# Another placing of the recurrence blocks and of ScalarE's and VectorE's work around them, in an mLSTM and MLP kernel

## The chip, the cores and the metric

One core of one Trainium2 chip runs the program. The metric is the device time of one execution in microseconds; the median of the runs counts. The profile is that of one execution, and its times are those of that execution.

## What is computed

A recurrence over 768 time steps for 4 batches and 8 heads (an mLSTM with exponential gates, a matrix memory C of 40 by 40 and a normalizer n for each head), and behind it an MLP with a SiLU gate on the 3072 tokens of 320 features, with 2048 hidden units:

```python
for t in range(S):                     # q, k, v: (4, 8, 768, 40)
    m_new = np.maximum(f_gate[:, :, t] + m, i_gate[:, :, t])
    f_stab = np.exp(f_gate[:, :, t] + m - m_new)
    i_stab = np.exp(i_gate[:, :, t] - m_new)
    C = f_stab * C + i_stab * einsum('bhd,bhe->bhde', v_t, k_t)
    n = f_stab * n + i_stab * k_t
    y[:, :, t] = sigmoid(o_gate_t) * (C @ q_t) / np.maximum(np.abs(n . q_t), 1.0)
x = y.transpose(0, 2, 1, 3).reshape(3072, 320)
h = x @ w_in                            # 320 x 2048
out = (h * sigmoid(h)) @ w_out          # 2048 x 320
```

## The kernel before

The recurrence is cut into 12 chunks of 64 time steps and 2 pairs of batches: 24 units of 128 tokens, in order. Unit n needs the state `Cm` of unit n-2. Three units make a step of 384 tokens, and there are eight steps. The MLP of a step goes through 16 groups of 128 hidden units. The main loop (line 1298) counts groups of all steps through, k = 18 to 128, with k // 16 the step and k % 16 the group.

In a turn k of that loop TensorE gets, in this order: the first product of group k (`first_product`: w_in by x, split into a high and a low part, so that a product is three products); a second product (`second_product`: the activations by w_out, in the same three parts) for groups four or more back; in an even turn the first product is cut in two and a second product lies between. All these matmuls use 64 rows of the array, and two of them on different row halves run beside each other: the first half of group k beside the second half of group k-1. Where two halves add to the same PSUM tile, one must have ended before the other starts. `relay` and `follow` see to that by a wait that passes through ScalarE's list: `relay` puts an empty instruction on ScalarE behind a matmul, `follow` makes a later matmul wait for it. `first_product` of turn k waits in that way for `rises[k - 2]`, the tanh of group k-2.

ScalarE and VectorE make the activations of group k-1 in turn k: `rise` (tanh `th` from the PSUM tile `spot`, line 916, on ScalarE; (th + 1) times `spot`, line 919, on VectorE, which frees that PSUM tile) and `part` (the high part `gh`, line 928, ScalarE; the low part `gl`, line 932, VectorE). `gh` and `gl` have four buffers each. There are three PSUM tiles called `spot`.

While a step's groups run, the three units of the next step are worked into it, each by a block at a given group (`PLACES`, line 41): in step 1 and later at groups 3, 7 and 11. `at[a]` in the loop is the unit whose block was `a` turns ago. In the block's own turn TensorE does, between the first and the second product, the scores of unit n+1 (line 570), the values of unit n (641, 658) and the state product of unit n (732), which takes the two free `spot` tiles. Then `close` (VectorE: `weigh` multiplies the scores of n+1, `norm` makes the denominators), `part`, `hold` (ScalarE copies the state product out as `pk`, line 761, and gives the two `spot` tiles back), `level` and `scale` (VectorE, which make x), `carry` step 0 (GpSimd), `turn_out` (VectorE transposes 32 by 32 blocks, line 798) and `turn_away` (SyncE starts four stores of x to DRAM, line 804). One turn later: `carry` step 1 (VectorE, four additions to `Cm`, line 792), and `turn`, in which SyncE starts the loads of unit n+3 (lines 476, 485, 505, 496) and of `lq` of unit n+2 (line 517) and GpSimd makes `am`. Two turns later: `add` (GpSimd), `misc` of unit n+1 (`gate` and `look` on ScalarE, lines 543 and 550, and `near` on GpSimd, line 554, which makes `qt`), and `turn_in` (SyncE loads x back transposed as `px`, line 812). Three turns later the exponential of unit n+2 (540) and `keys`. Six turns later, and for the third unit of a step four turns later, `xput`: ScalarE casts `px` to `xh` (841) and VectorE makes `xl` (842), which the first products of the next step read.

Each engine has its own list of instructions and they are in the order in which the code issues them (the order is written out by hand, there is no scheduler). The same holds for SyncE's DMA starts. The output of a step, three tiles of 128 tokens, is finished in groups 2 and 3 of the next step (`store`: ScalarE copies it out of PSUM, line 988, and SyncE starts two stores of it, line 993).

## Time and profile before

| | |
|---|---|
| time, median of 3 runs | 486.35 us (486.13 to 487.97) |
| the profiled execution | 488.12 us, of which the span (first to last instruction) is 486.3 us |
| TensorE, matmuls | 443.9 us busy (91% of the span) |
| VectorE | 292.6 us (60%) |
| ScalarE | 220.5 us (45%) |
| GpSimd | 124.0 us (26%) |

PE is TensorE's matmul row, ACT is ScalarE, DVE VectorE, POOL GpSimd, SP SyncE, and a q behind a name is the engine's queue of DMA starts. Up to about 84 us the kernel is in its first loop (step 0); then the main loop runs, with the starts of steps 2 to 7 at about 134, 195, 254, 314, 376 and 431 us. Step 7 holds no blocks. A line such as `[1.46 <-ACT pk L761]` says that the engine had been idle for 1.46 us and that the instruction of ScalarE on line 761 that writes `pk` ended the wait.

### The profile page before, as it was taken

To read this page: it belongs to the slowest core of one execution; us is meant where nothing else is said; L and a number is where in the kernel's file an instruction comes from. 1 tells how busy PE (TensorE), PEld (TensorE's weight loads), DVE (VectorE), ACT (ScalarE), POOL (GpSimd) and SP (SyncE) were. 2 spreads that over 40 slices of the span, in tenths; PEclk is the share of its full clock that TensorE was granted. 3 is DMA by queue.
4 is the path that set the end of the run, shared out by engine and by line. 5 is a ranking of instruction groups with operands and counts; after the bars stand their busy time and mean duration, and the time that the engine had idled before them with its cause. 6 is when DMAs were issued, how large, how long until landed. Compare 5 with 4: busy or idle time off the path is not lost.

```text
span 486.3 us, 16335 instructions
## 1 busy us (share of the span) xinstructions
PE 443.9 (91%) x6814; PEld 398.3 (82%) x6814; DVE 292.6 (60%) x647; ACT 220.5 (45%) x487; POOL 124.0 (26%) x136
## 2 busy tenths in 40 slices
PE   8999999999798996989969899798988989989996
PEld 5767777888698986989859888698977989989996
DVE  5798986678826675366652666536655355644342
ACT  7776677455623444233443334434424324434332
POOL 6733441343103441034410344104341031100000
PEclk9999999999979999899998999999979889999999
DMA  8999892255602646035650356604555031101001
GB/s 264 388 332 265 254 278 84 69 148 150 161 1 67 156 146 161 1 86 136 151 155 4 86 135 154 155 14 118 130 122 144 8 84 25 35 18 42 1 1 42
DMA packets 65402, 58.01 MB, mean 119 GB/s; under 512 B 33424, under 2 KB 51936, under 8 KB 65328
## 3 DMA queue, kind: packets, MB, share of 16 engines
q1 hardware_dynamic: 65056, 56.60, 42.5%
q8 instruction: 54, 0.88, 0.8%
q10 hardware_dynamic: 208, 0.26, 0.2%
q14 instruction: 20, 0.16, 0.1%
q0 software_dynamic: 64, 0.10, 0.1%
HBM read 49.28 MB, written 7.55 MB: 117 GB/s over the span
## 4 chain that ended last, share of the span: by engine, by line
PE 59%; issue 17%; ACT 8%; DVE 7%; DMA 7%; SPq 1%; POOL 0%; POOLq 0%; ACTq 0%; DVEq 0%
PE spot L1263 20%; PE pout L1285 17%; PE ph L885 6%; PE pout L967 5%; DMA px<-xd 4%; PE p L570 2%; DVE th L919 2%; ACT gh L928 2%; PE p L658 2%; DMA vb<-in_vp_dram 2%; PE spot L732 1%; PE p L641 1%; DVE Cm L792 1%; ACT th L916 1%; DMA D<-LFl 1%
## 5 line engine op out<-in xcount | busy, mean ns | idle before, releaser
L1263 PE MATMUL spot<-xh,wh 64*128 64x384 f32 x660 | 122.9, 363 | 28.8 <-ACT xh L841 17.6
L919 DVE SCALAR_TENSOR_TENSOR th<-th,spot 128x384 f32<-128x384 f32 x110 | 60.7, 552 | 80.7 <-ACT th L916 80.2
L916 ACT ACTIVATE th<-spot 128x384 f32<-128x384 f32 x110 | 53.7, 488 | 119.0 <-PE spot L1263 119.0
L1285 PE MATMUL pout<-woh,gh 64*128 64x320 f32 x648 | 106.7, 321 | 0.0
L1285 PE MATMUL pout<-wol,gh 64*128 64x320 f32 x648 | 104.6, 315 | 2.2 <-issue 1.3
L1285 PE MATMUL pout<-woh,gl 64*128 64x320 f32 x648 | 104.5, 314 | 0.0
L932 DVE TENSOR_TENSOR gl<-th,gh 128x384 fp32r<-128x384 f32 x112 | 66.0, 589 | 57.3 <-ACT gh L928 56.8
L928 ACT CAST gh<-th 128x384 fp32r<-128x384 f32 x112 | 57.4, 513 | 93.9 <-DVE th L919 66.5
L1263 PE MATMUL spot<-xl,wh 64*128 64x384 f32 x550 | 98.8, 348 | 0.9 <-issue 0.4
L1263 PEld LDWEIGHTS spot<-xh,wh 64*128 64x128 f32 x660 | 65.2, 191 | 40.1 <-ACT xh L841 19.2
L1263 PE MATMUL spot<-xh,wl 64*128 64x384 f32 x440 | 77.7, 344 | 0.0
L782 POOL TENSOR_TENSOR Cm<-Cm,lq 40x328 f32<-40x328 f32 x40 | 30.0, 751 | 149.6 <-PE p L658 148.0
L1285 PEld LDWEIGHTS pout<-wol,gh 64*128 64x128 f32 x648 | 65.2, 193 | 2.8 <-issue 1.6
L1285 PEld LDWEIGHTS pout<-woh,gh 64*128 64x128 f32 x648 | 64.9, 193 | 1.6 <-issue 0.7
L1285 PEld LDWEIGHTS pout<-woh,gl 64*128 64x128 f32 x648 | 65.1, 193 | 0.0
L554 POOL TENSOR_TENSOR qt<-qk,lq 104x512 f32<-104x512 f32 x22 | 29.1, 1323 | 124.5 <-ACT lq L550 112.8
L1263 PEld LDWEIGHTS spot<-xl,wh 64*128 64x128 f32 x550 | 55.5, 193 | 2.5 <-DVE xl L842 2.3
L1263 PEld LDWEIGHTS spot<-xh,wl 64*128 64x128 f32 x440 | 44.1, 193 | 0.0
L967 PE MATMUL pout<-wo,g 128*128 128x320 f32 x96 | 29.0, 436 | 0.0
L537 POOL TENSOR_TENSOR D<-D,am 128x512 f32<-128x512 f32 x20 | 26.8, 1339 | 6.5 <-DMA D<-LFd 4.5
L842 DVE TENSOR_TENSOR xl<-px,xh 128x384 fp32r<-128x384 f32 x18 | 18.8, 1043 | 13.6 <-ACT xh L841 13.6
L597 DVE TENSOR_TENSOR D<-p,D 128x512 f32<-128x512 f32 x24 | 16.5, 689 | 16.3 <-PE p L658 14.8
(160 smaller groups left out, 556.5 us busy)
## 6 DMA issues: line engine op xcount, KB each, us to landing
qk<-in_qk_dram SPq DMA_DIRECT2D x24, 512.0 KB, 5.3
ko<-in_ko_dram SPq DMA_DIRECT2D x24, 320.0 KB, 5.6
wro<-in_w_out_dram SPq DMA_DIRECT2D x8, 640.0 KB, 5.5
wri<-in_w_in_dram SPq DMA_DIRECT2D x8, 512.0 KB, 6.2
D<-LFl SPq DMA_DIRECT2D x32, 128.0 KB, 3.0
lq<-LFl SPq DMA_DIRECT2D x32, 128.0 KB, 5.0
vb<-in_vp_dram SPq DMA_DIRECT2D x48, 82.0 KB, 4.9
out_dram<-ob SPq DMA_DIRECT2D x45, 80.0 KB, 2.1
```

The costliest lines, as they stand in the source:

```text
L537: nc.gpsimd.tensor_tensor(out=self.Dm, in0=self.Dm, in1=self.am, op=ALU.add)
L554: nc.gpsimd.tensor_tensor(out=self.qt, in0=self.q[:KS], in1=self.lq[:KS], op=ALU.mult)
L782: nc.gpsimd.tensor_tensor(out=v, in0=v, in1=self.lq[r, :, L - 1].unsqueeze(2).broadcast_to([D, H, D1]), op=ALU.mult,)
L842: nc.vector.tensor_tensor(out=lo, in0=px[:, a, :], in1=hi.bitcast(F32), op=ALU.subtract)
L885: nc.tensor.matmul(ph, w, x, start=(i == 0), stop=(i == len(ops) - 1))
L916: self.tanh = nc.scalar.activation(th, ph, AF.Tanh, scale=0.5)
L919: nc.vector.scalar_tensor_tensor(out=th, in0=th, scalar=1.0, in1=ph, op0=ALU.add, op1=ALU.mult)
L928: nc.scalar.copy(gh, th)
L932: nc.vector.tensor_tensor(out=gl, in0=th, in1=gh.bitcast(F32), op=ALU.subtract)
L967: nc.tensor.matmul(self.po[t], g[:, ts], w, start=(fc == 0 and i == 0), stop=(last and i == len(ops) - 1), skip_group_check=(j == NSTEP - 1),)
L1263: m = nc.tensor.matmul(spot[g][:, :NT], *ops[i], start=(h == 0 and i == 0), stop=(h == 1 and i == n - 1), skip_group_check=True,)
L1285: m = nc.tensor.matmul(st.po[t], g[half(h), t * UT : (t + 1) * UT], w[half(h)], start=(f == 0 and i == 0 and (p, h) in ((0, 0), (0, 1), (1 ...
```

## The change

Seven things are changed.

- `PLACES`: from step 2 on the blocks lie at groups 1, 5 and 9, in step 1 still at 3, 7 and 11.
- `gh` and `gl` get five buffers instead of four.
- In `part`, `gl` is made ahead of `close`, and no longer behind it.
- Unit 8, the third of step 2, no longer goes through DRAM: it is left out of `AROUND`, so TensorE transposes its x in the turn after its block (`xpose`, line 830, three transposes) and `xput` follows at once.
- Work moves between turns. `misc` of unit n+1 goes from two turns after the block to the end of the block's own turn. `turn` and `add` follow in the next turn, directly behind `carry`, of which the first half now stands ahead of `part`. Stores 1 and 0 go ahead of `relay`, store 2 goes behind `part`. `turn_in` is issued ahead of `xput`.
- `first_product`: the wait for the tanh of group k-2 hangs on the first matmul of the second half (h = 1), and not on the first matmul of all.
- In the first even turn of a step's second product, five pieces of the first product stand ahead of it instead of four.

```diff
@@ -38,7 +38,7 @@
 NWT = 3
 
 EARLY = 7
-PLACES = ((5, 9, 12), (3, 7, 11))
+PLACES = ((5, 9, 12), (3, 7, 11), (1, 5, 9))
 FIRST = NFC + LAG
 LAST = NSTEP * NFC - 1
 
@@ -62,7 +62,7 @@
     cp = pool("cp", 1)
     p2 = pool("p2", 2)
     p3 = pool("p3", 3)
-    p4 = pool("p4", 4)
+    p5 = pool("p5", 5)
     pb = pool("pb", NBIG)
     pw = pool("pw", NWT)
     psO = pool("psO", 3, space=PSUM)
@@ -767,12 +767,12 @@
                 nc.scalar.copy(t[r, 1], self.pu[1][r])
             self.pu[1] = t[:, 1]
 
-        def carry(self, copy=nc.scalar.copy, steps=(0, 1)):
+        def carry(self, copy=nc.scalar.copy, steps=(0, 1), parts=(0, 1)):
             n, c, p = self.n, self.c, self.p
             if c == NC - 1:
                 return
             pu = self.pu
-            for a in range(2):
+            for a in parts:
                 r = slice(a * 64, a * 64 + D)
                 v = Cm[p][r, a, :].rearrange("p (h e) -> p h e", e=D1)
                 if c == 0:
@@ -895,7 +895,7 @@
                 next(x)
             if j == 0:
 
-                g = p4.tile([128, NT], F32, tag="gh", name=f"g{j}_{fc}")
+                g = p5.tile([128, NT], F32, tag="gh", name=f"g{j}_{fc}")
                 nc.vector.scalar_tensor_tensor(
                     out=g, in0=th, scalar=1.0, in1=ph, op0=ALU.add, op1=ALU.mult
                 )
@@ -908,7 +908,7 @@
                 out=th, in0=th, scalar=1.0, in1=ph, op0=ALU.add, op1=ALU.mult
             )
             self.th = th
-            self.part(fc, splits, between)
+            self.part(fc, splits, lambda: None, between)
 
         def rise(self, fc, splits):
             j, ph = self.j, spot[self.j * NFC + fc][:, :NT]
@@ -921,18 +921,19 @@
             )
             free.append(spot.pop(j * NFC + fc))
 
-        def part(self, fc, splits, between):
+        def part(self, fc, splits, between, ahead=lambda: None):
             j, th = self.j, self.th
-            gh = p4.tile([128, NT], F32R, tag="gh", name=f"gh{j}_{fc}")
-            gl = p4.tile([128, NT], F32R, tag="gl", name=f"gl{j}_{fc}")
+            gh = p5.tile([128, NT], F32R, tag="gh", name=f"gh{j}_{fc}")
+            gl = p5.tile([128, NT], F32R, tag="gl", name=f"gl{j}_{fc}")
             nc.scalar.copy(gh, th)
             for x in splits:
                 next(x, None)
-            between()
+            ahead()
             nc.vector.tensor_tensor(
                 out=gl, in0=th, in1=gh.bitcast(F32), op=ALU.subtract
             )
             self.g[fc] = (gh, gl)
+            between()
 
         def rows(self, fc, half):
 
@@ -994,7 +995,7 @@
 
 
     units = [Unit(n) for n in range(NU)]
-    AROUND = set(range(2 * UPS, NU))
+    AROUND = set(range(2 * UPS, NU)) - {3 * UPS - 1}
     free, spot = [], {}
     steps = {}
 
@@ -1203,7 +1204,7 @@
         j, fc = divmod(k, NFC)
         if j >= NSTEP - 1:
             return {}
-        return {fc - a: units[(j + 1) * UPS + u] for u, a in enumerate(PLACES[min(j, 1)])}
+        return {fc - a: units[(j + 1) * UPS + u] for u, a in enumerate(PLACES[min(j, 2)])}
 
     def splits(k):
         return [SPLITS[x[0]](int(x[1])) for x in LOWS.get(divmod(k, NFC), ())]
@@ -1267,8 +1268,9 @@
                     stop=(h == 1 and i == n - 1),
                     skip_group_check=True,
                 )
-                follow(m, turn)
-                turn = None
+                if h == 1:
+                    follow(m, turn)
+                    turn = None
         return m
 
     def second_product(p, k, turn=None):
@@ -1306,9 +1308,10 @@
             first_product(k, 0, 8, last_turn)
             last_turn = None
         elif even and ready:
-            first_product(k, 0, 4, rises[k - 2])
+            cut = 4 + (old % NFC == 0)
+            first_product(k, 0, cut, rises[k - 2])
             last_turn = relay(second_product(0, old, last_turn))
-            first_product(k, 4, 8)
+            first_product(k, cut, 8)
         else:
             first_product(k, 0, 8, rises[k - 2])
         new = steps[(k - 1) // NFC]
@@ -1318,13 +1321,15 @@
             rises[k - 1] = new.tanh
         if 0 in at:
             block(at[0].n)
+        last = steps[old // NFC] if ready and old % NFC == NFC - 2 else None
         if ready:
             m = second_product(1 if even else 2, old, last_turn)
             if 0 not in at:
+                if last:
+                    last.store(1 if even else 0)
                 last_turn = relay(m)
-            if old % NFC == NFC - 2:
-                for t in (1,) if even else (0, 2):
-                    steps[old // NFC].store(t)
+        if 1 in at:
+            at[1].carry(steps=(1,), parts=(0,))
         if k > FIRST:
             new.part((k - 1) % NFC, parts, (lambda: close(at[0].n)) if 0 in at else (lambda: None))
         if 0 in at:
@@ -1334,24 +1339,26 @@
             at[0].level()
             at[0].scale()
             at[0].carry(steps=(0,))
-            at[0].turn_out()
-            at[0].turn_away()
+            if at[0].n in AROUND:
+                at[0].turn_out()
+                at[0].turn_away()
+            if at[0].n + 1 < NU:
+                units[at[0].n + 1].misc()
+        if last and not even:
+            last.store(2)
         if 1 in at:
-            at[1].carry(steps=(1,))
-        if 2 in at and at[2].n + 1 < NU:
-            if at[2].n + 2 < NU:
-                units[at[2].n + 2].add()
-            units[at[2].n + 1].misc()
+            at[1].carry(steps=(1,), parts=(1,))
+            turn(at[1].n)
+            if at[1].n + 2 < NU:
+                units[at[1].n + 2].add()
         if 3 in at and at[3].n + 2 < NU:
             units[at[3].n + 2].exp()
             units[at[3].n + 2].keys()
-        if 1 in at:
-            turn(at[1].n)
+        if 2 in at and at[2].n in AROUND:
+            at[2].turn_in()
         for back in (4, 6):
-            if back in at and (at[back].n % UPS == UPS - 1) == (back == 4):
+            if back in at and at[back].n in AROUND and (at[back].n % UPS == UPS - 1) == (back == 4):
                 at[back].xput(steps[k // NFC + 1])
-        if 2 in at:
-            at[2].turn_in()
 
     st = steps[NSTEP - 1]
     st.mm2(NFC - 4)
```

## Rows read from the trace of the kernel before

**Rows 1.** The page: TensorE's busy time, share of the span and instructions.

```profile
PE 443.9 (91%) x6814; PEld 398.3 (82%) x6814; DVE 292.6 (60%) x647; ACT 220.5 (45%) x487; POOL 124.0 (26%) x136
```

**Rows 2.** Table of waits: engine, line, releaser: us in total, times, longest.

```profile
ACT gh L928 <- PE pout L1285: 26.0, 15, 2.5
...
PE spot L1263 <- ACT xh L841: 17.6, 6, 4.0
...
PE spot L1263 <- ACT pk L761: 9.8, 15, 1.5
...
ACT xh L841 <- DMA px<-xd: 5.7, 4, 1.7
...
PE spot L732 <- DVE th L919: 4.1, 6, 0.8
```

**Rows 3.** Timeline, TensorE, starts of steps 2, 4, 6: start, us, instruction [idle before].

```profile
134.14 0.69 PE L1263 MATMUL spot<-xh,wh 64*128 64x384 f32 x2 [2.85 <-ACT xh L841]
...
254.05 0.69 PE L1263 MATMUL spot<-xh,wh 64*128 64x384 f32 x2 [3.99 <-ACT xh L841]
...
375.79 0.59 PE L1263 MATMUL spot<-xh,wh 64*128 64x384 f32 x2 [2.15 <-ACT xh L841]
```

**Rows 4.** Busy time by stretch: length, PE, PEld, DVE, ACT, POOL (instructions), granted clock.

```profile
133.90:140.30 6.40, 6.16 (x40) 5.85 (x42) 1.11 (x2) 0.68 (x2) 0.00 (x0) 0.50 0.00 0
...
211.00:215.00 4.00, 3.98 (x48) 3.94 (x50) 2.83 (x7) 0.84 (x3) 1.67 (x2) 1.00 0.46 104
...
359.00:365.50 6.50, 5.92 (x40) 5.92 (x42) 2.36 (x7) 0.49 (x1) 2.55 (x3) 0.50 0.30 58
...
393.00:396.40 3.40, 3.40 (x26) 3.40 (x26) 2.75 (x6) 0.00 (x0) 0.66 (x1) 0.50 0.38 94
...
sum 15.50, PE 14.84 PEld 13.77 DVE 1.47 ACT 0.55 POOL 0.00; mean PE 3.71 PEld 3.44 DVE 0.37 ACT 0.14 POOL 0.00
```

**Rows 5.** Timeline, behind the first block of step 3.

```profile
209.61 0.77 ACT L988 ACTIVATE ob<-pout 128x320 f32<-128x320 f32 x2 [2.50 <-PE pout L1285]
...
210.26 0.51 ACT L928 CAST gh<-th 128x384 fp32r<-128x384 f32 x1
...
211.02 0.44 PE L1263 MATMUL spot<-xh,wh 64*128 64x384 f32 x2 [1.46 <-ACT pk L761]
```

**Rows 6.** Timeline, third block of step 3.

```profile
234.68 0.69 PE L570 MATMUL p<-qk 40*64 40x64 f32 x32
...
236.79 0.47 PE L732 MATMUL spot<-vb,kw 64*40 64x41 f32 x26 [0.67 <-DVE th L919]
...
238.82 0.44 PE L1263 MATMUL spot<-xh,wh 64*128 64x384 f32 x2 [0.22 <-ACT pk L761]
```

**Rows 7.** Timeline behind that block; below, the starts and landings of `lq`.

```profile
241.29 2.81 SPq L804 DMA_DIRECT2D xd<-xt  x4
...
241.48 0.49 ACT L916 ACTIVATE th<-spot 128x384 f32<-128x384 f32 x1 [2.52 <-PE spot L1263]
...
244.22 0.38 PE L1263 MATMUL spot<-xh,wh 64*128 64x384 f32 x2
...
249.22 0.55 SPq L812 DMA_DIRECT2D px<-xd  x1
...
253.49 0.51 ACT L841 CAST xh<-px 128x384 fp32r<-128x384 f32 x1 [1.71 <-DMA px<-xd]
...
L517 SPq DMA_DIRECT2D lq<-LFl x2: 602/604/607, 247.9 to 248.5; - x2
...
DMA to landing us min/median/max: 4.5/4.8/5.0
```

**Rows 8.** GpSimd's `qt` there; the durations of `xl`, ns, least, median, most.

```profile
246.93 1.30 POOL L554 TENSOR_TENSOR qt<-qk,lq 104x512 f32<-104x512 f32 x1 [5.13 <-DMA D<-LFl]
...
L842 DVE TENSOR_TENSOR xl<-px,xh x18: 551/1348/1366, 113.3 to 431.6; 128x384 fp32r<-128x384 f32 x18
```

**Rows 9.** TensorE's transposes in step 0: busy us, mean ns.

```profile
L830 PE MATMUL p<-ident,x 128*128 128x128 f32 x9 | 1.5, 273 | 0.0
```

## Prediction

> **What bounds the kernel now.** I read the page's engine times first: TensorE is busy for 91% of the span [rows 1], so what can be won is its idle time and the time in which it runs at the lower clock. The table of waits names the idle time [rows 2]: TensorE stood 17.6 us at six places for `xh` (once per start of a step from 2 on), 9.8 us at fifteen places for `pk` (the group behind each block waits for `hold`'s copies, which give back two PSUM tiles), and 4.1 us at six places inside blocks for `th` (the state products want the PSUM tile that `rise` frees). The timeline shows single waits: 2.85 at the start of step 2, 3.99 at that of step 4, 2.15 at that of step 6 [rows 3]. The table by stretch then shows the second half of the price: behind such a wait the granted clock is 0.50 (1.2 of 2.4 GHz) for 3 to 6 us, against 1.00 elsewhere, and 40 matmuls take 6.16 us where 48 take 3.98 [rows 4]. A half-clock stretch costs half its length: 3.1 us behind the start of step 2, 7.4 us in the four stretches 195 to 198.4, 253.6 to 259.1, 314.5 to 317.7 and 376 to 379.4 us together (the sum row: half of 14.84), 1.7 us at 393 us, where a 1.45 us wait for `pk` came before.
>
> **The change, part by part.** The sum is against the profiled execution (488.12 us, span 486.3). It stands 1.8 us above the median of 486.35; one stretch at 359 us, half clock for 6.5 us [rows 4], may belong to that execution alone, so I count nothing for it and take the sum off the median.
>
> *Waits behind blocks.* ScalarE's `gh` waited 26.0 us at fifteen places for second products [rows 2]: with four buffers it needs the one whose last reader is the second product queued behind the block. The fifth buffer's last reader ran two groups earlier. In the first block of a step two stores stand ahead of `gh` too (209.61, then `gh` 210.26), and TensorE waits 1.46 [rows 5]; in a third block 0.22 [rows 6]. From step 2 on the change moves the blocks away from the groups that store, and stores 0 and 1 now stand ahead of the relay in groups without a block. `pk` can then end before the second product does: 9.0 of 9.8 us go. The wait for `th` comes from a backlog of exponentials and x casts two groups ahead; part of that (`misc`) moves to another group: 2.0 of 4.1 us go, bounds 0 and 4.1.
>
> *Start of step 2.* Unit 8 leaves the way through DRAM (one DVE transpose, four stores, one load) for three TensorE transposes of 273 ns [rows 9], 0.8 us, and a wait for x and the cast that I bound by 0 and 2.85 us (the present wait) and take at 0.6: VectorE has `x` ready about when TensorE gets there, one group after the block. Removed: 2.85 and 3.1 of clock. Net 4.5 us gained.
>
> *Starts of steps 3 to 7.* They cost 17.6 - 2.85 = 14.75 us. With blocks at 1, 5, 9 the third unit's x is cast in group 13, not 15, so the starts themselves no longer wait. But ScalarE works its list in order, and the cast keeps its distance of four groups to the block while the DMA chain is as long as before: SyncE issues the four stores (241.29), seven loads and then `px` (249.22), and the cast starts at 253.49, after 1.71 us of waiting, 18.8 us after the block's first score matmul at 234.68 [rows 6, 7]. TensorE reached the end of that fourth group at 254.05 - 3.99 = 250.06 [rows 3], or 15.4 us after; without the 0.67 and 0.22 of rows 6 that is 14.5. It needs the tanh queued behind the cast at the first second-half matmul of group 15. A pair of groups takes 244.22 - 238.82 = 5.4 us [rows 6, 7], of which the even one, with two second products, has some 3.3: TensorE asks at 17.8 and gets the tanh at 18.8 + 0.51 + 0.49 = 19.8. That is a new wait of 2.0 us in group 15. ScalarE's four waits for `px` had a sum of 5.7, mean 1.4 [rows 2], and in step 5 there was none, so I take 1.5 us for each of steps 2 to 5 (bounds 0 and 3.0), and 0 in step 6, where no loads stand ahead of `px`. Net 14.75 - 6.0 = 8.75 us gained. The clock fell behind the start wait of 2.15 us and behind the 1.45 us before 393 us, but not behind the 1.46 us before 211 [rows 3 to 5]; so 1.5 us may go either way, and I keep half of the 7.4 us: 3.7 gained, and the 1.7 at 393 us.
>
> *`misc` two groups earlier.* ScalarE now does `gate` and `look` of unit n+1 at the end of block n. `look` needs `lq`, which was requested one group after block n-1: the second of its DMAs starts at 248.5 and lands up to 5.0 us later [rows 7], 18.6 to 18.8 us after the scores. Two pairs of groups and a block (10.8 + 2.5) separate two blocks and `look` comes 3.8 us into its block, so 17.1 us after the previous scores: it waits 1.5 us and ends 5.9 us into its block. The tanh queued behind it was due at 241.48 - 234.68 - 0.89 = 5.9, after 2.52 us of idle time [rows 6, 7]. So at the third block the idle time pays for it. At the second block two output DMAs now stand ahead of the loads in SyncE's queue, 0.6 us each like the `lq` issues of rows 7; the tanh is 1.2 us late, of which TensorE has 0.3 or 0.4 to spare: 0.8 us lost in each of four steps, 3.2 in all (bounds 0 and 10). All six output DMAs stand ahead of the first unit's `px`, 3.6 us; its cast comes six groups after its block, so this loses 0 to 2.4 us over the run; I take 1.0.
>
> *GpSimd beside VectorE.* `xl` takes 1.348 us in the median and 0.551 at best; it is long where `qt` runs on GpSimd (246.93) [rows 8]. The move frees `xl`, but `qt`, `am` and the addition now run beside `carry` and `gl`. I take 2.0 us lost over the run (bounds 0 and 10). The Trainium skill, "GPSIMD Engine Reference", section "8. Key points", says that the two engines share SBUF interfaces and that contention arises with VectorE instructions that have two SBUF inputs. The trace agrees for `xl`; by that rule `carry` and `gl` have the same exposure behind a block, which is the third rival.
>
> Priced at nothing: the cut of 5 instead of 4 (no wait stands there now), the wait hung on the first second-half matmul (one matmul sooner), the two halves of `carry` (the first fills VectorE's wait for `gh`), `gl` ahead of `weigh` (both start when the scores and `gh` are there; what follows shifts by under 0.4 us). If VectorE were full behind a block these would cost their 0.3 to 0.6 us each; it is the contention case.
>
> **Sum.** -9.0 - 2.0 - 4.5 - 8.75 - 3.7 - 1.7 + 3.2 + 1.0 + 2.0 = -23.5 us: 486.35 - 23.5 = 463.
>
> **Rivals.** *Hidden:* the loads land sooner relative to the groups, ScalarE never makes TensorE wait, the clock holds. Then 6.0, 3.7, 3.2, 1.0 and 2.0 come off as well: 447, or about 451 with some left. For: the spare is missed by 2 us in only one chain. Against: SyncE's issues are back to back in rows 7. *ScalarE waits longer:* 3.0 us in group 15 and 2 us at two blocks in four steps, the clock falling behind each group 15: 463 + 6 + 3.7 + 4 = 477. For: rows 7 make the wait likely; against: every TensorE delay gives the loads more time. *Contention:* each VectorE operation with two SBUF inputs waits behind one of GpSimd after a block, `gh` and the next tanh come 0.6 us late at 15 blocks: 463 - 2 + 9 = 470. *The waits only move:* the `pk` wait stays because tanh and `gh` become later, and group 15 takes the whole start wait: 486. *Slower:* three waits in each of steps 2 to 5 (second block, third block, group 15), all long enough that the half clock follows each. Twelve stretches at the mean of rows 4, 14.84 / 4 / 2 = 1.9 us, cost 22.3 instead of the 3.7 counted, and waits of 2.2 us each instead of 9.2 us in all cost 17 more: 499; with half the blocks spared 491. It decides if `lq` lands 1.5 us later than rows 7 say.
>
> **Chances.** The forecast 0.46, hidden 0.16, longer waits 0.15, contention 0.09, waits only move 0.06, slower 0.08. The range of 449 to 479 takes in the forecast, the contention, the longer waits and most of the hidden case. What this kernel's measurement can tell from no change is about 0.5% (2.4 us): faster 0.86, same 0.06, slower 0.08.
>
> **What would show it.** In the table of waits after: `spot` for `pk` near 1 us; `xh` no longer at step starts; a new TensorE wait for ScalarE's `th` in group 15 (1 to 2 us, four times) and a smaller one two groups behind the second block; ScalarE waiting for DMA at `look` and at `xh`; `xl` near 0.56 us; at 132 us no half clock. Wrong would be: `pk` waits of 1.4 us left, half clock in new places, or no ScalarE wait at group 13 (then the hidden case).

## The result and the profile after

The changed kernel takes 454.4 us in the median (452.9 to 454.9), the kernel before 486.2 beside it: a ratio of 0.934, with a 95% interval of 0.930 to 0.938. The forecast was 463 with a range of 449 to 479. The chip has a slower state that some executions fall into; the medians here take in such executions, the ratios leave them out. The profiled execution took 454.91 us, its span is 453.1. Lines have moved by one or two: the first product is L1264 now, the second L1287, the copy of the output L989.

TensorE's row of the page, to be held against [rows 1]:

```profile
PE 430.0 (95%) x6817; PEld 390.1 (86%) x6817; DVE 299.7 (66%) x646; ACT 224.4 (50%) x487; POOL 131.1 (29%) x136
```

The span is 33.2 us shorter. TensorE's idle time fell from 486.3 - 443.9 = 42.4 us to 453.1 - 430.0 = 23.1, which is 19.3 of them. Its busy time fell by 13.9, though the same products are made, so the clock comes next. Busy time by stretch: the two stretches of the main loop at half clock that are left, and the start of step 2, which ran at half clock before [rows 4] (columns as in rows 4):

```profile
184.00:187.80 3.80, 3.80 (x28) 3.80 (x30) 1.58 (x3) 1.32 (x3) 0.00 (x0) 0.55 0.00 0
225.00:228.80 3.80, 3.74 (x29) 3.74 (x30) 1.56 (x5) 0.99 (x2) 1.28 (x2) 0.56 0.17 28
```

```profile
132.00:138.00 6.00, 6.00 (x132) 5.75 (x129) 3.70 (x8) 2.98 (x6) 0.00 (x0) 1.00 0.00 0
```

Seven stretches of before held 6.16 + 14.84 + 5.92 + 3.40 = 30.3 us of matmuls at half speed [rows 4]; half of that, 15.2 us, is lost. Two are left, with 7.54 us at 0.55 of the clock, a loss of 3.4. So the clock gave 11.8 us, and 2.1 us are neither idle time nor clock. That last part shows in an undisturbed pair of groups: 5.35 us before, 5.30 after.

The table of waits, after (those of before are rows 2):

```profile
ACT xh L841 <- DMA px<-xd: 9.6, 3, 3.7
...
PE pout L1287 <- ACTq L1244: 6.7, 5, 2.3
...
ACT gh L928 <- PE pout L1287: 5.6, 6, 1.3
...
ACT lq L550 <- DMA lq<-LFl: 5.3, 3, 2.6
...
PE pout L1287 <- issue: 3.5, 4, 1.4
...
PE spot L1264 <- ACT pk L761: 0.5, 1, 0.5
PE spot L732 <- DVE th L919: 0.5, 1, 0.5
```

TensorE's waits for `xh` (17.6 us) are gone, those for `pk` fell from 9.8 to 0.5, those for `th` inside blocks from 4.1 to 0.5, and `gh` waits 5.6 us for second products instead of 26.0. Two lines are new. One is 6.7 us in which a second product waits for ScalarE's queue. That is the relay, an empty instruction behind which the second half may start. The other is ScalarE's wait for `px`, which was 5.7 us and is 9.6. They belong together, as the timeline at the end of step 2 shows:

```profile
183.90 0.51 ACT L841 CAST xh<-px 128x384 fp32r<-128x384 f32 x1 [3.70 <-DMA px<-xd]
...
183.98 0.63 PE L1287 MATMUL pout<-woh,gh 64*128 64x320 f32 x2 [2.30 <-ACTq L1244]
```

ScalarE stood 3.70 us before the cast of `px`. The relay of the second product stands behind the cast in its list, and TensorE stood 2.30 us, to 0.08 us after the cast began. The clock fell to half right there. The same pair stands at 293.46 and 293.54 (3.04 and 1.64 us) and at 346.95 and 347.03 (2.89 and 1.49), with the clock at 1.00 behind them. In step 3 there is none.

The second block of step 5 shows the other new wait, and what follows it:

```profile
320.62 0.63 ACT L550 ACTIVATE lq<-lq 104x512 f32<-104x512 f32 x1 [2.60 <-DMA lq<-LFl]
...
320.70 0.42 PE L1287 MATMUL pout<-woh,gh 64*128 64x320 f32 x2 [0.96 <-ACTq L1244]
...
321.38 1.30 POOL L554 TENSOR_TENSOR qt<-qk,lq 104x512 f32<-104x512 f32 x1 [3.03 <-ACT lq L550]
...
322.14 1.82 DVE L792 TENSOR_TENSOR Cm<-Cm,pk 40x164 f32<-40x164 f32 x2
...
322.65 1.13 POOL L529 TENSOR_TENSOR am<-mask,aT 128x512 f32<-128x512 f32 x1
...
323.85 1.73 POOL L537 TENSOR_TENSOR D<-D,am 128x512 f32<-128x512 f32 x1
...
324.46 1.56 DVE L792 TENSOR_TENSOR Cm<-Cm,pk 40x164 f32<-40x164 f32 x2
...
326.05 0.56 DVE L919 SCALAR_TENSOR_TENSOR th<-th,spot 128x384 f32<-128x384 f32 x1
...
326.63 0.51 ACT L928 CAST gh<-th 128x384 fp32r<-128x384 f32 x1 [2.85 <-DVE th L919]
...
326.71 0.42 PE L1287 MATMUL pout<-woh,gh 64*128 64x320 f32 x2 [0.33 <-ACTq L1244]
```

ScalarE waited 2.60 us for `lq`, TensorE 0.96 behind it. Then GpSimd runs `qt`, `am` and the addition to `D` without a break, and beside them VectorE's four additions of `carry` take 1.82 + 1.56 us where four take 1.15 when nothing runs beside them (b1, at 286.46). `th` and `gh` come late (`gh` stood 2.85 us), and TensorE stands another 0.33.

### The profile page after: what moved, and what is told of

Its sections match the earlier page's. It is cut to its first block, busy times and chain, and to the rows that moved or that the text cites. A ratio compares the mean times of both kernels' runs of the same rounds, so it can differ in the third digit from the quotient of the medians.

```text
span 453.1 us, 16196 instructions
## 1 busy us (share of the span) xinstructions
PE 430.0 (95%) x6817; PEld 390.1 (86%) x6817; DVE 299.7 (66%) x646; ACT 224.4 (50%) x487; POOL 131.1 (29%) x136
## 4 chain that ended last, share of the span: by engine, by line
PE 58%; issue 20%; DVE 10%; DMA 7%; ACT 2%; SPq 1%; POOL 0%; POOLq 0%; ACTq 0%; DVEq 0%
PE pout L1287 19%; PE spot L1264 18%; PE ph L885 7%; PE pout L968 6%; DVE Cm L792 4%; DMA px<-xd 3%; PE p L570 3%; PE p L658 2%; DVE th L919 2%; PE p L641 2%; DMA qk<-in_qk_dram 2%; PE spot L732 1%; DVE gl L932 1%; DMA ko<-in_ko_dram 1%; DMA lq<-LFl 1%
## 5 line engine op out<-in xcount | busy, mean ns | idle before, releaser
L1264 PE MATMUL spot<-xh,wh 64*128 64x384 f32 x660 | 138.7, 343 | 0.5 <-ACT pk L761 0.5
L1287 PE MATMUL pout<-woh,gh 64*128 64x320 f32 x648 | 121.0, 318 | 7.1 <-ACTq L1244 6.7
L1287 PE MATMUL pout<-woh,gl 64*128 64x320 f32 x648 | 117.1, 308 | 3.5 <-issue 3.5
L1287 PE MATMUL pout<-wol,gh 64*128 64x320 f32 x648 | 116.5, 307 | 1.6 <-DVE wol L337 1.6
L1264 PE MATMUL spot<-xl,wh 64*128 64x384 f32 x550 | 114.2, 338 | 0.0
L1264 PEld LDWEIGHTS spot<-xh,wh 64*128 64x128 f32 x660 | 89.6, 186 | 3.4 <-ACT th L916 1.3
L1264 PE MATMUL spot<-xh,wl 64*128 64x384 f32 x440 | 90.7, 336 | 0.0
L1287 PEld LDWEIGHTS pout<-woh,gh 64*128 64x128 f32 x648 | 78.0, 186 | 13.5 <-ACTq L1244 9.2
L1287 PEld LDWEIGHTS pout<-woh,gl 64*128 64x128 f32 x648 | 78.2, 186 | 2.8 <-issue 2.8
L1287 PEld LDWEIGHTS pout<-wol,gh 64*128 64x128 f32 x648 | 78.0, 186 | 1.9 <-DVE wol L337 1.9
L1264 PEld LDWEIGHTS spot<-xl,wh 64*128 64x128 f32 x550 | 70.2, 186 | 0.0
L1264 PEld LDWEIGHTS spot<-xh,wl 64*128 64x128 f32 x440 | 58.1, 186 | 0.0
L792 DVE TENSOR_TENSOR Cm<-Cm,pk 40x164 f32<-40x164 f32 x70 | 42.0, 634 | 0.5
L885 PE MATMUL ph<-x,wi 128*128 128x384 f32 x64 | 23.7, 492 | 0.3 <-DVE wi L301 0.3
## 6 DMA issues: line engine op xcount, KB each, us to landing
D<-LFl SPq DMA_DIRECT2D x32, 128.0 KB, 3.1
lq<-LFl SPq DMA_DIRECT2D x32, 128.0 KB, 4.9
```

What stands on the lines that cost most here:

```text
L792: nc.vector.tensor_tensor(out=w, in0=w, in1=pu[d][r], op=ALU.add)
L885: nc.tensor.matmul(ph, w, x, start=(i == 0), stop=(i == len(ops) - 1))
L1264: m = nc.tensor.matmul(spot[g][:, :NT], *ops[i], start=(h == 0 and i == 0), stop=(h == 1 and i == n - 1), skip_group_check=True,)
L1287: m = nc.tensor.matmul(st.po[t], g[half(h), t * UT : (t + 1) * UT], w[half(h)], start=(f == 0 and i == 0 and (p, h) in ((0, 0), (0, 1), (1 ...
```

## The experiments

All times are medians; a ratio is to the kernel before on the same chip, whose median there was 485 to 487 us. 0.01 of ratio is 4.9 us. Where a kernel isn't set against the changed one on the same chip, the ratios are compared (0.934 for the changed kernel in both of its measurements).

The table below is worked out from the start times of TensorE's timeline. It gives the time from the first second-product matmul of one even turn to that of the next, in us, summed over steps 2 to 5, so four pairs of groups in each column; the column's number is the first group of the pair within its step. An undisturbed pair gives 4 x 5.30 = 21.2, or 21.4 at 5.35. With the new places the blocks lie in columns 0, 4 and 8 and the px cast in 12 and 14; with the old ones the blocks lie in 2, 6 and 10 and the start of the next step in 14.

```
kernel              0     2     4     6     8    10    12    14    sum
before           27.0  36.8  21.4  32.1  22.2  38.4  23.2  40.5  241.7
b1_places_alone  32.6  21.4  33.0  21.6  38.0  22.2  25.8  22.2  216.8
changed kernel   30.6  21.9  33.5  23.8  35.3  22.2  21.2  29.2  217.7
e0_after_again   30.3  21.9  33.9  24.0  35.1  22.1  21.2  26.9  215.4
e1_places        24.4  30.7  23.5  30.5  28.2  34.6  21.1  43.2  236.2
e2_four_buffers  32.7  21.9  33.4  24.6  38.6  21.2  21.4  37.8  231.5
e3_unit8_dram    30.0  21.8  32.1  24.1  34.9  21.7  21.2  26.5  212.3
e4_misc_later    30.6  21.9  30.8  21.7  33.0  22.0  23.4  24.9  208.2
e5_px_first      30.5  21.9  34.3  23.8  34.5  22.6  21.2  21.2  210.0
e6_lq_first      31.1  21.9  31.5  22.2  32.1  24.6  21.2  27.9  212.4
e7_both          30.6  21.9  30.9  22.7  32.8  22.3  21.2  21.2  203.5
e8_first_wait    29.9  22.1  31.5  24.6  35.8  22.5  21.6  29.9  218.0
e10_near_later   30.5  21.9  31.5  23.4  33.3  22.6  21.2  26.7  211.1
e11_queue_near   31.0  21.9  29.7  23.1  32.7  22.9  21.2  21.2  203.7
```

**e0, the changed kernel again**, no edit.

> The changed kernel once more, unaltered, as the base for the runs beside it. Both theories of the unexplained TensorE waits speak on it. Theory 1: the waits that the profile of after puts down to issue (155.78, 210.24, 225.06, 264.51 us) belong to places in TensorE's instruction list, at which the next piece of the list is fetched, so they come back at the same places in the list within 1 us, with 0.8 to 1.4 us each, and the time is 454 +- 1.5. Theory 2: they are chance, and stand elsewhere or nowhere.

Measured: 452.9 us (451.5 to 458.2), ratio 0.935 (0.927 to 0.942), so the result holds on a second chip. Of the four waits put down to "issue" that the first theory names, three came back at the same places of TensorE's list of instructions (0.55, 0.80 and 1.29 us), 4 to 5 us earlier in time; that of 155.78 shrank to 0.10 us, and two of 0.65 and 0.52 came at other places. So the places hold and the sizes don't; more on them in the last section.

**e1, the places undone.**

```diff
-PLACES = ((5, 9, 12), (3, 7, 11), (1, 5, 9))
+PLACES = ((5, 9, 12), (3, 7, 11), (3, 7, 11))
         if last and not even:
+            if 0 in at:
+                last.store(0)
             last.store(2)
```

> The changed kernel with the blocks of step 2 and later back at groups 3, 7 and 11; store 0 then goes behind part in the block's turn, so that nothing stands ahead of gh. Theory: the groups of the blocks are what empties the starts of steps 3 to 7. Then TensorE again waits 3 to 4 us at the starts of steps 3 to 5, 2 and 1.4 us at the last two, with 3 to 5 us of half clock behind each of the first three, while the waits for pk stay away: 454 + 13 less the 5.4 us of waits in group 14 = 463 to 469. Rival: the order of ScalarE's and VectorE's work did most of it, and the starts wait under 1.5 us each: 455 to 458.

Measured: 478.6 us, ratio 0.985 (0.979 to 0.994), 25.6 us above the changed kernel beside it and so more than expected. Table of waits:

```profile
PE spot L1264 <- ACT xh L841: 18.5, 5, 5.2
...
ACT xh L841 <- DMA px<-xd: 11.5, 4, 3.8
```

The starts of steps 3 to 7 wait 18.5 us again (17.6 before, with that of step 2), and the clock is at half behind four of them, 20.5 us in all; a fifth stretch of 3.4 us, at 128.0, lies behind a wait for weights (1.91 us at 127.04). The waits for `pk` stay away.

**e2, four buffers.**

```diff
-    p5 = pool("p5", 5)
+    p5 = pool("p5", 4)
```

> The changed kernel with four buffers of gh and gl instead of five. Theory: the fifth buffer takes away what was left of the wait for pk once no store stood ahead of gh. gh waits again for the second product behind the block at fifteen places, pk ends 0.2 us too late each time: 3 us, and x is 0.4 us later: 456.5 to 459. Rival 1: the fifth buffer did all of it, and 1.4 us come back at each block: 470 or more. Rival 2: it did nothing, 454 +- 1.

Measured: 469.5 us, ratio 0.965 (0.960 to 0.971), 16.6 us above the changed kernel: far more than the theory gave and at the edge of the rival's time. Table of waits:

```profile
ACT gh L928 <- PE pout L1287: 40.9, 20, 3.6
...
DVE gl L932 <- PE pout L1287: 32.3, 15, 3.1
...
ACT xh L841 <- DMA px<-xd: 15.9, 4, 4.6
PE pout L1287 <- ACTq L1244: 14.9, 12, 3.3
...
PE spot L1264 <- ACT pk L761: 3.2, 13, 0.5
```

`pk` takes only 3.2 us of it. The damage is in ScalarE's and VectorE's lists: `gh` waits 40.9 us for a free buffer. VectorE's `gl` waits 32.3 us for second products too, at fifteen places, and since it now stands ahead of `close`, everything that makes x stands behind that wait (in b1, with four buffers and the old order, such waits of `gl` are 0.7 us). x leaves later, ScalarE's wait for `px` grows from 9.6 to 15.9 us, TensorE's wait for the relay from 6.7 to 14.9, and the clock falls in four places. In the table of pairs 11.9 of the 13.8 us against the profiled run of the result are in column 14, the px cast, and column 8, the third block.

**e3, unit 8 through DRAM again.**

```diff
-    AROUND = set(range(2 * UPS, NU)) - {3 * UPS - 1}
+    AROUND = set(range(2 * UPS, NU))
```

> The changed kernel with unit 8 on the way through DRAM again, its cast in group 15. Theory: the start of step 2 waits again for that cast, 2.5 to 4 us, and 3 us go to the half clock behind it, less the 0.8 us of the transposes: 459 to 461. Rival: with misc out of the way the loads are in time, and it is within 1 us of 454.

Measured: 452.2 us, ratio 0.929 (0.924 to 0.933), no slower than the changed kernel (452.9), and so the rival's time. The wait came back, but not its price. TensorE's timeline at the start of step 2:

```profile
132.76 0.45 PE L1264 MATMUL spot<-xh,wh 64*128 64x384 f32 x2 [1.82 <-ACT xh L841]
```

After 1.82 us of idle time the clock stayed at 1.00, where it had fallen around the 2.85 us of before [rows 3, 4], and what the start lost was not to be found in the total.

**e4, `misc` later.**

```diff
             if at[0].n in AROUND:
                 at[0].turn_out()
                 at[0].turn_away()
-            if at[0].n + 1 < NU:
-                units[at[0].n + 1].misc()
@@
+        if 2 in at and at[2].n + 1 < NU:
+            units[at[2].n + 1].misc()
         if 3 in at and at[3].n + 2 < NU:
```

> The changed kernel with one part undone: `misc` of unit n+1 (`gate` and `look` on ScalarE, `qt` on GpSimd) goes back from the end of the block's own turn to two turns behind the block. Theory (the early `misc` costs ScalarE a wait for `lq` at the second block, but empties the turn two behind the block): TensorE's waits of 0.96 and 0.33 us behind the second block of step 5 go (-1.3 us), `xl` takes 1.35 us again beside `qt`, and the waits for `th` inside blocks come back in part (+1 to +3.5): 454 to 457 us in sum, 0 to 2 us above the changed kernel (453 to 454.4). Rival (the early `misc` is a loss by itself, as the prediction priced it, 3.2 us against 2.0 for th): 450 to 452.

Measured: 446.8 us, ratio 0.920 (0.915 to 0.924): 0.0145 below the changed kernel, some 7 us. That `misc` was moved is a loss in this kernel, as the rival says, and a larger one than the rival's. Groups of instructions (busy us and mean ns behind the bar) of the changed kernel, and then of this one:

```profile
L792 DVE TENSOR_TENSOR Cm<-Cm,pk 40x164 f32<-40x164 f32 x70 | 42.0, 634 | 0.5
```

```profile
L792 DVE TENSOR_TENSOR Cm<-Cm,pk 40x164 f32<-40x164 f32 x70 | 22.6, 358 | 0.5
...
L842 DVE TENSOR_TENSOR xl<-px,xh 128x384 fp32r<-128x384 f32 x17 | 18.4, 1081 | 15.4 <-ACT xh L841 15.4
```

With `qt` two turns later the additions of `carry` take 22.6 us instead of 42.0, and it is `xl` that is long, 18.4 us instead of 9.4. But TensorE doesn't wait for `xl`. The waits for `th` inside blocks return (3.4 us), as they were before. In the table of pairs the gain is in the blocks (columns 4 to 8, 7.1 us against the profiled run of the result) and in column 14 (4.3), and 2.2 are given back in column 12. Which part of the early `misc` costs this, e6 tells better than this run.

**e5, `px` ahead of the loads.** Behind a third unit SyncE starts the load of x first, and those of units n+3 and n+2 after it.

```diff
-    def turn(n):
+    def tail(n):
+        return n in AROUND and n % UPS == UPS - 1
+
+    def fetch(n):
         if n + 1 >= EARLY and n + 3 < NU:
             units[n + 3].load()
         if n + 2 < NU:
             units[n + 2].load_q()
+
+    def turn(n):
+        if not tail(n):
+            fetch(n)
+        if n + 2 < NU:
             units[n + 2].shift()
@@
             at[2].turn_in()
+            if tail(at[2].n):
+                fetch(at[2].n)
```

> The changed kernel with one edit: behind the third unit of a step SyncE issues the load of x (`px`) ahead of the loads of unit n+3 and of `lq`, no longer behind them. Theory (ScalarE's cast at group 13 waits for `px` because the seven loads stand ahead of it in SyncE's queue; TensorE's waits of 2.30, 1.64 and 1.49 us behind it, and the half clock of 184 to 187.8 us, come from that): `px` lands 4 to 5 us sooner, ScalarE's waits for it (9.6 us) and TensorE's (5.4 us) go, half clock -1.9: 446 to 449 us. Rival 1 (the stores and the transfer bound the landing, not the place in the queue): waits stay, 453 to 455. Rival 2 (the loads, now later, make `look` or the products of unit n+3 late): a new wait for `lq` or `qk` behind the first block of the next step, 451 to 456.

Measured: 447.8 us, ratio 0.921 (0.916 to 0.926), 0.013 or 6.5 us below the changed kernel, as the theory says. SyncE's DMA starts behind the third block of step 5, in the changed kernel (its score matmuls started at 329.42) and here (323.11):

```profile
335.18 2.44 SPq L804 DMA_DIRECT2D xd<-xt  x4
337.72 1.10 SPq L476 DMA_DIRECT2D D<-LFl  x2
...
343.44 0.55 SPq L812 DMA_DIRECT2D px<-xd  x1
```

```profile
328.87 1.87 SPq L804 DMA_DIRECT2D xd<-xt  x4
332.18 0.38 SPq L812 DMA_DIRECT2D px<-xd  x1
332.65 2.05 SPq L476 DMA_DIRECT2D D<-LFl  x2
```

`px` is requested 9.1 us after the scores, not 14.0. ScalarE's waits for it are gone, those of TensorE for the relay fell from 6.7 to 1.4 us, and all four pairs of column 14 are undisturbed (21.2).

**e6, `lq` first.** In `turn`, `load_q` of unit n+2 is moved ahead of `load` of unit n+3.

```diff
     def turn(n):
+        if n + 2 < NU:
+            units[n + 2].load_q()
         if n + 1 >= EARLY and n + 3 < NU:
             units[n + 3].load()
         if n + 2 < NU:
-            units[n + 2].load_q()
             units[n + 2].shift()
```

> The changed kernel with one edit: in `turn` SyncE issues the loads of `lq` of unit n+2 ahead of the loads of unit n+3, not behind. Theory (`look` waits 2.0 to 2.6 us for `lq` at the second block because five other loads stand ahead of it): ScalarE's wait for `lq` (5.3 us at three places) goes, TensorE's 1.3 us behind the second block of step 5 too: 1 to 2 us below the changed kernel, 451.5 to 453. Rival (the place in the queue doesn't decide, or TensorE has the spare anyway): within 0.5 us of the changed kernel.

Measured: 450.0 us, ratio 0.928 (0.923 to 0.933), some 3 us below, with intervals that overlap. The trace is clearer: the wait of `look` for `lq` is gone from the table of waits, and columns 4 and 8 lose 2.0 and 3.2 us, of which column 10 gives back 2.4. The run also bears on e4. Its line of the additions to `Cm`:

```profile
L792 DVE TENSOR_TENSOR Cm<-Cm,pk 40x164 f32<-40x164 f32 x70 | 38.0, 577 | 0.5
```

The additions are still long (38.0 us, against 42.0 in the changed kernel and 22.6 in e4), yet columns 4 to 8 take 85.8 us, as in e4 (85.5), and not 92.6. So what the early `misc` costs TensorE there goes away with the wait for `lq`, and additions that are long without that wait cost TensorE little. Some 2 to 3 of these 7 us are something else again: waits put down to "issue" are 4.6 us in these columns of the changed kernel, 2.2 here and 1.3 in e4.

**e7, both edits of the queue.**

> The changed kernel with both edits of the queue: the load of x ahead of the loads of the next units behind a third unit, and `lq` ahead of the other loads everywhere. Theory: the two gains add, since they lie in different groups (13 and 5): 445 to 448 us, ratio 0.915 to 0.922 to the kernel before; TensorE's waits for ScalarE's queue below 1 us in sum. Rival (the waits taken away are followed by the next limit, the waits for instructions or the two row halves): 450 to 453.

Measured: 440.8 us, ratio 0.907 (0.903 to 0.912), 13 us below the changed kernel and below the theory's range. The two gains add up to some 9.5; that the sum is better by another 3.5 lies within the noise of three ratios, each known to 0.004 or 0.005 either way. TensorE's longest lines in the table of waits:

```profile
PE pout L1295 <- issue: 2.9, 3, 1.5
...
PE pout L1295 <- DVE wol L337: 1.6, 1, 1.6
```

Of the waits for ScalarE's queue one of 0.3 us is left, and `px` and `lq` hold up ScalarE nowhere behind step 1. What is left from step 2 on is mostly "issue".

**e10, `qt` alone later.** `gate` and `look` stay at the end of the block's turn, `near` goes back by two turns.

```diff
-                units[at[0].n + 1].misc()
+                units[at[0].n + 1].gate()
+                if units[at[0].n + 1].c > 0:
+                    units[at[0].n + 1].look()
@@
+        if 2 in at and at[2].n + 1 < NU and units[at[2].n + 1].c > 0:
+            units[at[2].n + 1].near()
```

> The changed kernel with one third of `misc` moved back: GpSimd's `qt` (`near`) two turns behind the block, while ScalarE's `gate` and `look` stay in the block's own turn. It tells apart why the kernel with the whole of `misc` moved back took 446.8 us. Theory (`qt` pushes GpSimd's `am` and addition to `D` into the time of VectorE's `carry`, whose additions to `Cm` then take 1.4 instead of 0.32 us: 42.0 us for 70 of them against 22.6): the additions come back to about 23 us, `xl` goes up to 18 us, and most of the 6.5 us are gained: 447 to 450 us. Rival (ScalarE's waits for `lq` behind the block, 5.3 to 5.7 us, are what it costs): 452 to 454, with the additions at 23 us all the same.

Measured: 449.6 us, ratio 0.923 (0.918 to 0.929), 0.011 or some 5 us below the changed kernel, in the range of the theory. But the additions fell only half the way, to 33.0 us, and `xl` stayed short. GpSimd's timeline shows why:

```profile
246.95 1.04 POOL L529 TENSOR_TENSOR am<-mask,aT 128x512 f32<-128x512 f32 x1
248.07 1.30 POOL L537 TENSOR_TENSOR D<-D,am 128x512 f32<-128x512 f32 x1
249.33 1.30 POOL L554 TENSOR_TENSOR qt<-qk,lq 104x512 f32<-104x512 f32 x1
```

Its `lq` was long there, so `qt` ran at once behind the addition to `D`, in the same burst as before, last instead of first. An instruction that is issued later and finds nothing to wait for does not run later. In e4 it was ScalarE's later `look` that held it back. ScalarE still waits 6.8 us for `lq`, at seven places. So taken alone the run speaks for the contention, with a part of the effect for a part of the cause: `qt` no longer stands ahead of `am` and the addition to `D` when `lq` is late. But in e6 the additions are longer (38.0 us), `lq` is in time, and the blocks are faster: the two runs together speak for the late `lq` and what it pushes behind it as the cost, rather than for the length of the additions.

**e11, both edits of the queue and `qt` later.**

> The kernel with both edits of SyncE's queue (440.8 us) and `qt` two turns later. Theory (contention behind the block costs TensorE time through `gl`, `th` and the relays, independent of the queue): the additions to `Cm` at 23 us instead of 38, 2 to 5 us below the former: 436 to 439, ratio 0.898 to 0.906. Rival (with the queue in order nobody waits for VectorE any more): 440 to 441.

Measured: 439.5 us, ratio 0.904 (0.900 to 0.909). The additions take 35.4 us instead of 38.1. It can't be told from e7 (0.907, 0.903 to 0.912): the rival, that nobody waits for VectorE once the queue is in order, isn't refuted. With 2.7 us less of additions it isn't a strong test, and the whole of `misc` two turns later wasn't tried with the queue in order. Either kernel is faster than the changed one by about 3%.

**b1, the places alone**, in the kernel before.

```diff
-PLACES = ((5, 9, 12), (3, 7, 11))
+PLACES = ((5, 9, 12), (3, 7, 11), (1, 5, 9))
-        ... enumerate(PLACES[min(j, 1)])}
+        ... enumerate(PLACES[min(j, 2)])}
```

> The kernel before with the new places alone (blocks at groups 1, 5, 9 from step 2 on), everything else as it was. Undone alone they cost 25.6 us. Theory (the places carry the gain at the step starts, but with four `gh` buffers and the old order the groups behind the blocks still wait for `pk`): the waits at the starts (17.6 us) and the half clock behind them go, new ones of 1 to 2 us come in group 15, the `pk` waits fall from 9.8 to some 5 us since the first block's stand no longer behind the stores: 465 to 472 us, ratio 0.956 to 0.970. Rival (the places need the other parts: without them the waits only move into groups 13 to 15): 478 to 487.

Measured: 458.7 us, ratio 0.944 (0.939 to 0.949): 27.6 of the change's 32 us, far more than either theory gave. Table of waits:

```profile
ACT gh L928 <- PE pout L1285: 33.8, 17, 2.9
...
ACT xh L841 <- DMA px<-xd: 4.8, 4, 1.6
...
PE spot L732 <- DVE th L919: 4.1, 6, 0.8
...
PE spot L1263 <- ACT pk L761: 3.6, 15, 0.5
...
PE spot L1263 <- ACT th L916: 2.7, 6, 0.6
...
PE spot L1263 <- ACT xh L841: 2.4, 1, 2.4
```

With four buffers and the old order, `gh` waits longer than before (33.8 against 26.0 us), yet TensorE's wait for `pk` is 3.6 us, not 9.8. Only the start of step 2 still waits for `xh`. TensorE's waits for `th` lie in group 13, behind a long `xl`; behind the px cast it waits once, 0.22 us at 349.62. From the first pair of step 2 to the end of the span, the profiled run of b1 takes 319.5 us, that of the changed kernel 320.0 (steps 2 to 5: 216.8 and 217.7; the rest: 102.8 and 102.3) and e0 317.7: there, the other six edits together gained nothing in one execution and 1.8 us in the other. The rest of their gain lies ahead of step 2, whose first pair starts at 136.7 in b1, 133.2 in the changed kernel and 132.0 in e0. Without the early `misc` the same stretch takes 310.1 us (e4, in an execution 3.0 us below its median): one of the six takes back most of what the others give. The timelines of step 5 show another part of where their gain went. In b1 the scores of the third block start at 330.93, the cast of `px` 18.6 us later at 349.55, and TensorE asks for the relay 18.5 us after the scores (349.62 less the wait). In the changed kernel the scores start at 329.42 and the cast 17.5 us later (346.95), but TensorE asks after 16.1 (347.03 - 1.49). It gets to group 14 2.4 us sooner, the load only 1.1, and the rest is waited away.

**e8, the wait on the first matmul again.**

```diff
-                if h == 1:
-                    follow(m, turn)
-                    turn = None
+                follow(m, turn)
+                turn = None
```

> The changed kernel with the wait for the tanh of group k-2 back on the first matmul of a group instead of the first of its second half. The prediction priced that part at nothing. Theory (the wait there lets the row halves of two groups run one matmul apart: an undisturbed pair of groups took 5.35 us before and 5.30 after): 0.05 us for each of 53 pairs, and each wait behind the px cast one matmul longer: 2 to 4 us above the changed kernel, pairs at 5.35 again. Rival (the 0.05 us come from something else, such as the order of `gl`): pairs at 5.30, within 1 us of the changed kernel.

Measured: 455.3 us, ratio 0.937 (0.932 to 0.942), 0.003 above the changed kernel, which the intervals don't separate. The undisturbed pairs are unmistakable: in steps 6 and 7 they take 5.35 us, as in the kernel before, or 5.33, against 5.27 to 5.32 in the changed one. So this wait is what sets the 0.05 us, and for the 48 pairs of steps 2 to 7 that makes 2.4 us, near the 2.1 that the account of the result left over.

## Why the prediction was right, and where its steps failed

The forecast of 463 us lay 8.6 above the result. Its sum had -15.0 us of idle time and -8.5 of clock; measured were -19.3 and -11.8, and the 2.1 of the pairs. The chain was right: the starts no longer wait, the clock holds behind them, and a smaller wait for the x cast takes their place. That the total came this near is in part luck: the gains in idle time and clock were too small, and so was the price of the early `misc`.

*Waits behind blocks, -9.0.* They fell by 9.3. The size is right and the cause is half wrong. The step gave two reasons: the fifth buffer frees `gh`, and the blocks leave the groups that store. The places do most of it: b1 has four buffers and a longer wait for `gh`, and still loses 6.2 of the 9.8 us: no group behind a block waits over 0.54 us there, where it was 1.46 behind two stores [rows 5]. With the new order and four buffers (e2) `pk` waits 3.2 us, so the buffer takes some 3. What it is worth in this kernel, 16.6 us, is mostly that the new order can't do without it, and this wasn't in the sum at all: I had put "`gl` ahead of `weigh`" at nothing, which holds with five buffers only. (The 32.3 us that `gl` waits in e2 say so; `gl` behind `close` with four buffers wasn't tried in this kernel.)

*Waits for `th`, -2.0.* They fell by 3.6 (bounds 0 to 4.1), and by the move of `misc`: with it undone they are 3.4 again.

*Start of step 2, -4.5.* The wait and the half clock are gone, but e3 shows that the transposes are not what it takes. With unit 8 in DRAM the wait is 1.82 us, the clock holds and the total isn't longer. In b1, without the other parts, the wait is 2.4 us and the clock falls.

*Starts of steps 3 to 7, -14.75 + 6.0.* The starts wait no more, and the place of the new wait is one turn off: not the tanh in group 15 but the relay in group 14, which stands behind the same cast in ScalarE's list. I had looked only for the instruction whose result TensorE needs, and missed an empty one in the same queue. The sum, 5.4 us of the 6.7 (three steps at 2.30, 1.64, 1.49), is near the 6.0; in e0 it is 4.3 us at four steps. That SyncE's order makes it, the seven loads ahead of `px`, was the reason in the prediction, and e5 confirms it: without them the waits go. In b1 the same chain costs TensorE 0.2 us, as it comes to group 14 later: a wait of this kind takes back what the blocks gain.

*Clock, -3.7 - 1.7 - 3.1.* This term was too small by 3.3. I kept half of the 7.4 us for 1.5 us waits; two waits of this size (1.64 and 1.49) left the clock at 1.00. And the stretch at 359 us, which I had left out as a thing of that execution, didn't come back: 5.92 / 2 = 3.0 us. One of the prediction's own signs of being wrong did come, half clock in new places: at 184 behind the new wait, at 225 behind a wait for instructions. Both together cost 3.4 us.

*`misc` earlier, +3.2, and contention, +2.0.* Together with the -2.0 for `th` the move was priced at +3.2; e4 gives about +7. The waits for `lq` came as told, though not in each of the four steps: ScalarE's at three second blocks (1.96, 0.79 and 2.60 us), TensorE's behind it at one (0.96, then 0.33). The contention on VectorE came as well: of the 70 additions to `Cm` the 30 with nothing of GpSimd's beside them took 0.31 to 0.33 us each, the other 40 up to 1.45, and all together 19.4 us more than before (42.0 against 22.6). That this costs TensorE time isn't shown: with `lq` in time, e6 keeps 38.0 us of additions and is as fast in the blocks as e4. By the Trainium skill's rule in the prediction ("GPSIMD Engine Reference", "8. Key points") `carry` and `gl` are exposed. The trace agrees for `carry`, 634 ns against 359 in the mean; for `gl` it doesn't, 571 against 589: of the 20 that ran beside GpSimd 17 kept their 0.54 to 0.56 us, and three took 1.15. The rival "contention" was thus right that VectorE is held up, but the loss that it priced at fifteen blocks isn't shown.

*Six output DMAs, +1.0.* ScalarE's waits for `px` after step 2 are all at third units: 0.

*Priced at nothing.* The wait on the first matmul of the second half is worth the 0.05 us of each pair. The cut of 5, the order of the stores and the halves of `carry` can't be told apart here; none was tried alone.

*A sum of the rivals.* For *Slower* with half of its eight waits at blocks spared, 499 - 4 x (1.9 + 2.2) gives 483 us, not 491. Nothing else hangs on it.

## What to carry to other kernels

Where a wait passes through an engine's list, all that stands behind the delayed instruction waits with it, empty instructions too: go through the list, not only through the results. Look then at the order of the DMA queue that feeds it: two edits that put the load with the earliest reader first gained 13 us in a kernel that had just gained 32. And test the parts of a bundle alone: here one part of seven carried 27.6 of 32 us, and one was a loss of about 7 as the queue stood.

## What the runs showed of the hardware

**Waits for instructions.** TensorE's timeline of the changed kernel, two of the waits put down to "issue", where no semaphore held it:

```profile
210.24 0.41 PE L1287 MATMUL pout<-woh,gl 64*128 64x320 f32 x2 [0.88 <-issue]
...
225.06 0.42 PE L1287 MATMUL pout<-woh,gl 64*128 64x320 f32 x1 [1.41 <-issue]
```

Counting TensorE's instructions (weight loads, matmuls and its own semaphore instructions) from the first, the waits of over 0.25 us that are put down to "issue" in the main loop stand at the same place of every 256, remainder 193 or 194, in every run of this case. The trace of the changed kernel has 53 packets of 16384 bytes on the instruction queue, one for each 256 of its 13707 instructions. For the three of before and the four longest of the changed kernel, the start of the nearest earlier 16384-byte packet on that queue (q8 on the page):

```
kernel   wait ends  us     instruction  mod 256   16384-byte packet from
before   287.60     0.39    8385        193       285.08
before   359.58     1.35   10690        194       356.81
before   389.87     0.33   11458        194       387.19
changed  155.78     0.98    4546        194       153.06
changed  210.24     0.88    6337        193       207.60
changed  225.06     1.41    6849        193       222.33
changed  264.51     1.33    8130        194       261.82
```

Each ends 2.5 to 2.8 us after such a packet began. So these look like waits for the next piece of the list; no run changes the fetching itself. They come in and behind blocks, where instructions go quickly: in the changed kernel the 194 instructions up to such a wait took 1.9 to 4.7 us, wait included, against 7.7 in the median of all pieces. The longest are 2.28 us (e11, at 218 us, with the clock at half for 3.4 us behind it) and 2.05 (e8). The half clock at 359 us in [rows 4] lies at one of these, too. The Trainium skill, "Runtime: NRT & Kernel Launch", section "Instruction fetch mechanics", says that instructions come in 16 KiB blocks of 256 and that crossing a block is mostly hidden. The trace agrees on the size; it was hidden at most blocks and cost 0.3 to 2.3 us at some.

**The clock.** It was at half (0.50) behind waits of 2.30 us (184), 2.45 (b1, 134.98) and 1.41 (225), and at 1.00 behind 1.82 (e3, 132.76), 1.64 (293.54) and 1.49 (347.03). In b1 it was at half from 227.1 to 230.5 with no wait over 0.67 us in the ten before. Here the length of the wait alone doesn't tell.
